# Centring three of four token tiles on GpSimd, and turning them one batch later

## The chip, the cores and the metric

The kernel runs on one core of one Trainium2 chip. The metric is the device time of one execution in microseconds (us); of several executions the median is taken. The engines are TensorE (PE in the profile; its weight loads are PEld), VectorE (DVE), ScalarE (ACT), GpSimd (POOL) and SyncE (SP), which issues the transfers.

## The reference

One transformer-like block over 2048 tokens of width 512. The tokens are normalised without gain or bias, then go two ways: through sliding-window attention (32 heads of 16, each query sees itself and the 255 tokens before it) and through a gated feed-forward of width 1792. The two are multiplied and added to the input.

```python
def _layernorm(x, axis=-1, eps=1e-5):
    m = jnp.mean(x, axis=axis, keepdims=True)
    v = jnp.var(x, axis=axis, keepdims=True)
    return (x - m) / jnp.sqrt(v + eps)
...
    xn = _layernorm(x, axis=-1)
    s = _A_ref(xn, A_wqkv, A_wo)
    g = _silu(_B_ref(xn, B_w1, B_w3, B_w2))
    return x + s * g
```

## The kernel before, in words

The 2048 tokens are worked on in four tiles of 512 (`t` = 0 to 3), each of four blocks of 128 tokens. For precision, operands of the large products are held as a high and a low float16 part, and three products are summed (high by high, high by low, low by high). Splitting a float32 array is shared out: ScalarE scales it (L342) and copies the high part (L343), and GpSimd subtracts to get the low part, in two halves of 256 columns (`halves`, L336 to L339). GpSimd makes so the low parts of the feed-forward weights, of the hidden values (L1050 and L1051, read by the down products of L1242), and of the attention output.

Before a tile can be used, its tokens are prepared (`prepare`, L425). For each block, `stats` (L435) takes mean and variance on VectorE. `rstd` (L440) makes the reciprocal root for all four blocks: three short operations on VectorE, then, for the second to fourth tile, ten on GpSimd (L463 to L472). `centre` (L474) subtracts the mean and multiplies with the reciprocal root, in place, one 128x512 operation of VectorE a block (L475). For the first tile `turn` (L478) then transposes on TensorE. For the others `turn_beside` (L502) does: each block is turned in two pieces, each piece a few small matmuls against an identity (L513) into free columns of a PSUM bank that a score matmul is using anyway, from which VectorE copies the high part (L522) and subtracts the low part (L523).

The attention's work is cut into 32 units (`units`), two for each of 16 pairs of tile and group of eight heads, and each unit into five batches (`batches`, L1427). A batch holds score matmuls of a first pass (L661), whose row maxima VectorE takes (L675), and score matmuls of a second pass (L741), to which VectorE adds masks (L748) and of which ScalarE takes the exponential (L751). Between batches, `spread` (L1456) lays the dense work: gate and up products (L1017), projections (L593), values (L563), down products (L1242 or, in the last two tiles, L1160), and the output projection (L1294).

What sets the order: TensorE issues in the order in which the program is written. The other engines' instructions are put in order at build time by a scheduler, from priorities and from when it thinks their inputs are there; `tc.issue_after` ties instructions behind one of the same engine. On the chip each engine's queue is first in, first out.

The preparation of tiles 2 to 4 is spread over batches. `prepare_beside` (L529) makes a list `work`: statistics (in pairs of blocks for the second tile, one block at a time for the others), the reciprocal roots, then the centring in the same portions, then `turns`. The list goes into `behind`, and each batch takes one entry (L1449 to L1451), tied behind the batch's last row maximum if it is on VectorE. `turns` is called twice, once from this list and once by a call outside it, and the second of the two calls puts the eight turning pieces of the tile into `besides`. From there `part` of the first pass (L650) takes them, as a rule one for a batch, and more than one while the units of the first three pairs of tile and group run.

Buffers of 512 float32 columns come from a pool of 55 slots (`take` and `give`); a token block's slot is given back when its second piece has been turned (L515).

Of the kernel before, what the change touches and what calls it, by code (L numbers as in the profile page):

```python
# [15 lines left out]
ALU = mybir.AluOpType  # L16
# [67 lines left out]
def tile_block(ctx: ExitStack, tc: tile.TileContext, x, wqkv, wo, w1, w3, w2, out):  # L84
    nc = tc.nc
# [58 lines left out]
    def later(n, f):  # L144
        made_so_far[0] += 1
        queue.append((now[0] + n, made_so_far[0], f))
# [274 lines left out]
    lasts = {}  # L421
# [3 lines left out]
    def prepare(t):  # L425

        mv = lnpool.tile([P, 4, 2], F32, name="mv")
        rs = lnpool.tile([P, 4], F32, name="rs")
        xts = {}
# [42 lines left out]
            pool.tensor_mul(rs[:, b0:b1], sq, r0)  # L472

        def centre(b):  # L474
            lasts["centre"] = nc.vector.tensor_scalar(xts[b], xts[b], mv[:, b, 0:1], rs[:, b:b + 1],  # L475
                                                      op0=ALU.subtract, op1=ALU.mult)

        def turn(b):  # L478
            if t not in X:
# [22 lines left out]
        def turn_beside(b, n, s):  # L502
# [15 lines left out]
            def rest():  # L518
# [5 lines left out]
                if n:  # L524
                    turned[t] = turned.get(t, 0) + 1
            return rest
        return load, stats, rstd, centre, turn if t == 0 else turn_beside

    def prepare_beside(t, more=0):  # L529


        load, stats, rstd, centre, turn = prepare(t)
        made = [(0, lambda b=b: load(b)) for b in range(4)]
        pairs = [(0, 1), (2, 3)] if t == 1 else [(b,) for b in range(4)]
        work = [lambda bs=bs: [stats(b) for b in bs] for bs in pairs]
        work.append(lambda: rstd(0, 4))
        work += [lambda bs=bs: [centre(b) for b in bs] for bs in pairs]
        ready = []

        def turns():  # L540

            ready.append(0)
            if len(ready) == 2:
                besides.extend(lambda s, b=b, n=n: turn(b, n, s) for b in range(4) for n in (0, 2))
        work.append(turns)
        made.append((0, lambda: later(more, lambda: behind.extend(work))))
        return made, turns
# [296 lines left out]
    def load(t, f):  # L844
        if t:
            a = [take(F16) for _ in range(2)]
            WF[t, f] = [a, None]
            for k in range(2):
                lasts["load"] = nc.sync.dma_start(a[k], dW1[f, k])
            return  # L850
        RAW[f] = raw = [take(F32) for _ in range(2)]
        for k, w in enumerate((w1, w3)):
            lasts["load"] = nc.sync.dma_start(raw[k].rearrange("p (c f) -> p c f", f=P),
                              w[:, f * P:(f + 1) * P].rearrange("(c p) f -> p c f", p=P))
# [475 lines left out]
    def feed_forward():  # L1330
# [4 lines left out]
        for t in range(NT):  # L1335
            for f in range(FB):
# [27 lines left out]
                if f == FB - 4 and t + 2 < NT:  # L1364
                    first, second = prepare_beside(t + 2, 8)
                    pieces += first
# [214 lines left out]
    for n in range(len(units)):  # L1581
        t = n // 8
# [8 lines left out]
        b = n % 8 - (2 if t < 3 else 3)  # L1591
# [6 lines left out]
    for n, u in enumerate(units):  # L1598
        if n == 0:
            first, second = prepare_beside(1, 2)  # L1600
            later(10, lambda: run(first[:4]))
        if n == 1:
            run(first[4:])
            second()
        if n == 6:
            wout[0]()
        if n == 7:
            wout[1](2)
            beside_scores(12, lambda s: then(s, wout[2](s), lambda: later(2, lambda: wout[3](2)), lambda: later(3, out_scale)))
        want += a_unit - other[n]  # L1610
        mine = more(want)

        lists = in_groups(beside[n]), in_groups(mine)
        both = sorted([((i + 0.5) / len(l), k, i) for k, l in enumerate(lists) for i in range(len(l))])
        spread(batches(n, u, units[n + 2] if n + 2 < len(units) else None), [piece for _, k, i in both for piece in lists[k][i]])
        k = n // 2 + 2
        if n % 2 == 0 and k < len(tiles):
            later(1, lambda k=k: fetch(*tiles[k]))
# [33 lines left out]
```

## Time and profile before

| | |
|---|---|
| runs of the kernel | 818.03, 820.48 and 822.88 us; median 820.48 us |
| the profiled execution | 817.94 us, of which the span of the profile is 816.1 us |
| granted clock of TensorE | 0.998 of full speed |
| TensorE busy | 98% of the span, 9176 matmuls |
| VectorE, ScalarE, GpSimd busy | 78%, 48%, 45% |

The profile shows one execution. Its views name an instruction by engine, line of the kernel, operation, and tiles written and read. A timeline gives, for each instruction or each run of like ones, its start and its duration in us, and in brackets how long the engine stood idle before it and whom it was waiting for. Since one instruction can begin while the one before it writes its last results, the durations of neighbours overlap a little. The chain of work that ended last is followed back from the end: at each step to what released the instruction, or to the one before it on its engine. A table of windows gives the busy time of each engine within a stretch.

### The profile page before, as it was taken

What the parts mean: (1) busy time and instruction counts of PE and PEld (TensorE: products, weight loads), DVE (VectorE), ACT (ScalarE), POOL (GpSimd) and SP (SyncE); (2) the same over time, 40 slices, a digit from 0 to 9 for tenths busy, and PEclk for the clock granted to TensorE, in tenths of its full rate; (3) what the DMA queues carried; (4) which work ended last, traced back from release to release, by engine and by line L of the source; (5) the groups of instructions that cost most, each with busy time, mean ns of one, the idle gap of its engine ahead of it and who ended that gap; (6) DMA issues with size and microseconds to landing.
All of it is one profiled execution on the core that took longest, in us unless ns stands there. A gap on an engine that the chain in (4) does not pass through costs nothing.

```text
span 816.1 us, 23926 instructions
## 1 busy us (share of the span) xinstructions
PE 796.3 (98%) x9176; PEld 404.3 (50%) x9176; DVE 633.0 (78%) x2033; ACT 395.1 (48%) x595; POOL 371.0 (45%) x656
## 2 busy tenths in 40 slices
PE   8998989999999999999999999999999999999997
PEld 4443444444444444444444454456544654466464
DVE  8787688888898767787988888777677886875537
ACT  6879486563536544345444334344344234344411
POOL 2237266232329536344444355530246376650671
PEclk9999999999999999999999999999999999999999
DMA  9979665664742486747536362755553653325511
GB/s 283 257 246 309 211 192 169 202 209 146 217 137 85 133 251 196 232 132 217 160 124 186 91 185 82 210 153 151 165 151 85 169 160 109 88 72 178 159 37 64
DMA packets 109923, 134.71 MB, mean 165 GB/s; under 512 B 18736, under 2 KB 64752, under 8 KB 109808
## 3 DMA queue, kind: packets, MB, share of 16 engines
q1 hardware_dynamic: 109520, 132.66, 55.0%
q8 instruction: 72, 1.18, 0.6%
q10 hardware_dynamic: 288, 0.52, 0.2%
q14 instruction: 43, 0.35, 0.1%
HBM read 91.75 MB, written 37.09 MB: 158 GB/s over the span
## 4 chain that ended last, share of the span: by engine, by line
PE 71%; DVE 13%; ACT 6%; DMA 4%; issue 3%; POOL 2%; SPq 0%; DVEq 0%; POOLq 0%; ACTq 0%
PE m L1017 27%; PE m L1242 8%; PE po L769 7%; PE m L1160 7%; PE m L593 6%; PE s L741 5%; DVE junk L675 4%; PE m L1294 3%; PE m L563 3%; PE s L661 2%; DVE s L748 2%; PE po L661 1%; ACT slot L342 1%; ACT pt L751 1%; ACT slot L343 1%
## 5 line engine op out<-in xcount | busy, mean ns | idle before, releaser
L1017 PE MATMUL m<-XH,slot 128*128 128x512 f16 x896 | 267.3, 380 | 1.5 <-DVE slot L614 1.0
L751 ACT ACTIVATE pt<-s,es 128x1024 f32<-128x1024 f32 x152 | 167.7, 1114 | 195.3 <-DVE s L748 191.3
L339 POOL TENSOR_TENSOR slot<-slot,slot 128x256 f16<-128x256 f32 (+1 forms) x178 | 117.8, 691 | 207.1 <-ACT slot L1050 77.9
L1017 PEld LDWEIGHTS <-slot 128*128 128x128 f16 x1344 | 124.8, 98 | 155.6 <-issue 11.9
L1017 PE MATMUL m<-XL,slot 128*128 128x512 f16 x448 | 169.8, 379 | 0.0
L748 DVE TENSOR_TENSOR s<-s,MK 128x256 f32<-128x256 f32 (+2 forms) x280 | 118.7, 434 | 49.9 <-PE s L741 46.3
L675 DVE CUSTOM_DVE_ANT_0 junk<-s,MW 128x320 bf16<-128x320 f32 x276 | 133.9, 485 | 17.7 <-PE s L661 11.2
L675 DVE CUSTOM_DVE_ANT_0 junk<-po,MW 128x320 bf16<-128x320 f32 x172 | 83.4, 485 | 4.3
L1242 PE MATMUL m<-slot,slot 128*128 128x512 f16 x336 | 80.9, 386 | 2.5 <-POOL slot L339 2.1
L769 PE MATMUL po<-pt,V 64*32 64x320 f32 (+4 forms) x2880 | 77.2, 342 | 0.8 <-DVE pp L304 0.8
L593 PE MATMUL m<-XH,slot 128*128 128x512 f16 x240 | 70.9, 380 | 1.2 <-DVE slot L614 0.6
L1160 PE MATMUL m<-slot,slot 128*128 128x256 f16 x588 | 68.4, 273 | 0.3 <-DVE slot L1036 0.3
L1075 POOL TENSOR_TENSOR slot<-slot,slot 128x256 f16<-128x256 f32 x98 | 65.2, 678 | 1.2
L1032 ACT ACTIVATE slot<-m,sgs 128x512 f32<-128x512 f32 x56 | 38.3, 683 | 54.8 <-PE m L1017 44.2
L1160 PEld LDWEIGHTS <-slot 128*128 128x128 f16 x588 | 56.2, 98 | 11.8 <-issue 3.1
L769 PEld LDWEIGHTS po<-pt,V 64*32 64x32 f32 x2880 | 50.4, 106 | 23.2 <-PE s L513 0.9
L1036 DVE SCALAR_TENSOR_TENSOR slot<-slot,m 128x512 f32<-128x512 f32 x56 | 38.3, 684 | 29.7 <-ACT slot L1032 29.7
L741 PE MATMUL s<-qa,KA 50*64 50x320 f16 (+3 forms) x1472 | 58.6, 259 | 0.5 <-DVE os L784 0.2
L593 PEld LDWEIGHTS <-slot 128*128 128x128 f16 x384 | 35.7, 98 | 44.5 <-issue 3.2
L741 PEld LDWEIGHTS <-KA 50*64 50x64 f16 x1472 | 30.3, 105 | 52.2 <-issue 30.8
L339 POOL TENSOR_TENSOR on<-on,rb 128x256 f32<-128x256 f32 x32 | 24.4, 785 | 61.3 <-DMA rb<-de 48.1
L1242 PEld LDWEIGHTS <-slot 128*128 128x128 f16 x336 | 31.1, 99 | 42.6 <-issue 9.8
(188 smaller groups left out, 1120.7 us busy)
## 6 DMA issues: line engine op xcount, KB each, us to landing
slot<-dW SPq DMA_DIRECT2D x98, 256.0 KB
slot<-in_B_w_dram SPq DMA_DIRECT2D x56, 256.0 KB
slot<-dFold SPq DMA_DIRECT2D x48, 256.0 KB
dW<-slot SPq DMA_DIRECT2D x42, 256.0 KB
slot<-in_A_x_dram SPq DMA_DIRECT2D x30, 256.0 KB
KA<-dK SPq DMA_DIRECT2D x24, 288.0 KB
qa<-dQ SPq DMA_DIRECT2D x32, 192.0 KB
slot<-dWQ SPq DMA_DIRECT2D x24, 256.0 KB
```

The source lines that it names most:

```text
L339: op(out[:, c], a[:, c], b[:, c])
L593: nc.tensor.matmul(cell["pp"], w[:, (a * NC + c) * P:(a * NC + c + 1) * P], b[:, c, :], start=(c, i) == parts[0][0], stop=(c, i) == parts[ ...
L675: lasts["maximum"] = nc.vector.tensor_tensor_reduce(out=junk[:, :n], in0=s[:, r, :n], in1=mask, scale=1.0, scalar=NEG, op0=ALU.add, op1=AL ...
L741: nc.tensor.matmul(s[64 * h:64 * h + 64, r, o:o + 64 * n], ka[rows, 2 * p + a, 64 * (m + 4):64 * (m + 5)], qa[rows, 2 * p + a, 64 * (m + k ...
L748: nc.vector.tensor_add(v, v, MK[:, kind, of:of + n, :].unsqueeze(1).to_broadcast([P, 2 * len(which), n, 64]))
L751: lasts["exp"] = nc.scalar.activation(pt, s, AF.Exp, scale=es)
L769: nc.tensor.matmul(cell["po"][32 * i:32 * i + 32, h, 64 * (m + k):64 * (m + k + n)], V[64 * h:64 * h + 64, (4 * t + m // 2) % VB, hd * VW: ...
L1017: nc.tensor.matmul(cell[k], w[:, (a * NC + c) * P:(a * NC + c + 1) * P], b[:, c, :], start=c == 0 and i == 0, stop=c == NC - 1 and i == 2)
L1032: nc.scalar.activation(sg, cell[0], AF.Tanh, scale=sg_scale[:, f:f + 1])
L1075: nc.gpsimd.tensor_sub(lo, view, hi)
L1160: nc.tensor.matmul(cell["ps"][:, c], made[:, f:f + P], wj[:, g:g + 256], start=j == j0 and c == 0 and n == 0, stop=j == j1 - 1 and n == 2, ...
L1242: nc.tensor.matmul(ps, hh[:, a * TW + b * P:a * TW + (b + 1) * P], w[:, c * D:(c + 1) * D], start=f == f0 and i == 0, stop=f == f1 - 1 and ...
```

## The change

For the second to fourth tile (`t` of 1 to 3) `centre` is issued on GpSimd in place of VectorE, as two operations of 256 columns for each block: 24 operations of 128x256 in place of 12 of 128x512. The first tile keeps VectorE. And the list `work` gets an entry that does nothing, between the last centring and `turns`, so that the turning pieces are offered one batch later.

```diff
         def centre(b):
-            lasts["centre"] = nc.vector.tensor_scalar(xts[b], xts[b], mv[:, b, 0:1], rs[:, b:b + 1],
-                                                      op0=ALU.subtract, op1=ALU.mult)
+            if t == 0:
+                lasts["centre"] = nc.vector.tensor_scalar(xts[b], xts[b], mv[:, b, 0:1], rs[:, b:b + 1],
+                                                          op0=ALU.subtract, op1=ALU.mult)
+                return
+            for c in (slice(0, 256), slice(256, 512)):
+                nc.gpsimd.tensor_scalar(xts[b][:, c], xts[b][:, c], mv[:, b, 0:1], rs[:, b:b + 1],
+                                        op0=ALU.subtract, op1=ALU.mult)
...
         work += [lambda bs=bs: [centre(b) for b in bs] for bs in pairs]
+        work.append(lambda: None)
         ready = []
```

## The prediction

> **What bounds the kernel now.** I read the page first: the engines' busy time, then the chain of work that ended last.
>
> ```profile
> span 816.1 us, 23926 instructions
> ...
> PE 796.3 (98%) x9176; PEld 404.3 (50%) x9176; DVE 633.0 (78%) x2033; ACT 395.1 (48%) x595; POOL 371.0 (45%) x656
> ...
> PE 71%; DVE 13%; ACT 6%; DMA 4%; issue 3%; POOL 2%; SPq 0%; DVEq 0%; POOLq 0%; ACTq 0%
> ```
>
> TensorE is busy for 796.3 of 816.1 us. The change takes nothing from TensorE, so all that it can win lies in the 19.8 us in which TensorE stands idle, and only in those of them that the centring causes. The chain has 13% of VectorE, so somewhere VectorE sets the pace. To find where, I took the busy time by windows (columns: window and its length, then PE, PEld, DVE, ACT and POOL busy with counts, clock, DMA share, GB/s), and then TensorE's timeline, keeping the instructions with idle time before them.
>
> ```profile
> 115.00:120.00 5.00, 3.54 (x32) 1.50 (x24) 4.86 (x20) 4.03 (x10) 1.51 (x4) 1.00 0.65 202
> 120.00:125.00 5.00, 3.99 (x64) 2.31 (x64) 3.93 (x17) 5.00 (x9) 4.30 (x7) 1.00 0.77 260
> 125.00:130.00 5.00, 4.36 (x55) 2.14 (x53) 4.16 (x12) 3.94 (x11) 2.07 (x4) 1.00 0.63 218
> 130.00:140.00 10.00, 9.18 (x151) 4.89 (x150) 9.16 (x37) 7.22 (x11) 5.98 (x10) 1.00 0.52 164
> 140.00:160.00 20.00, 20.00 (x258) 10.06 (x257) 15.31 (x58) 9.72 (x18) 5.69 (x11) 1.00 0.54 177
> 160.00:180.00 20.00, 18.64 (x160) 8.22 (x166) 17.07 (x64) 14.69 (x23) 10.93 (x18) 1.00 0.65 215
> ...
> 395.00:425.00 30.00, 29.95 (x387) 14.12 (x392) 26.82 (x87) 14.41 (x18) 10.15 (x24) 1.00 0.43 125
> ```
>
> ```profile
> 116.53 0.22 PE L694 MATMUL s<-identh,NM 64*64 64x64 f16 x2 [1.09 <-DVE NM L688]
> ...
> 118.62 0.59 PE L593 MATMUL m<-XH,slot 128*128 128x512 f16 x2 [0.37 <-DVE slot L1036]
> ...
> 121.44 0.30 PE L661 MATMUL s<-KA,qa 48*64 48x256 f16 x4 [1.01 <-ACT pt L751]
> ...
> 127.47 0.33 PE L661 MATMUL po<-KA,qa 48*64 48x320 f16 x4 [0.64 <-DVE XL L523]
> ...
> 133.34 2.04 PE L769 MATMUL po<-pt,V 64*32 64x320 f32 x72 [0.82 <-DVE pp L304]
> ...
> 190.39 1.46 PE L1242 MATMUL m<-slot,slot 128*128 128x512 f16 x6 [0.40 <-DVE slot L614]
> ```
>
> Between 115 and 134 us TensorE loses 1.09 + 0.37 + 1.01 + 0.64 + 0.82 = 3.93 us, nearly all on VectorE's account. This is where the second tile's tokens are prepared. From 140 to 160 us TensorE is never idle, from 160 to 180 us it loses 1.36 us, and one wait of 0.40 us follows at 190.39 us. Now the centring itself: its summary over the run (durations as least, median and most, in ns), VectorE's timeline around the second and third tile's, and the summary for the fourth tile's four.
>
> ```profile
> L475 DVE TENSOR_SCALAR slot<-slot,mv,rs x16: 535/544/1102, 9.5 to 421.4; 128x512 f32<-128x512 f32 x16
> ```
>
> ```profile
> 109.64 0.87 DVE L475 TENSOR_SCALAR slot<-slot,mv,rs 128x512 f32<-128x512 f32 x1 [0.40 <-POOL rs L472]
> ...
> 110.51 0.82 DVE L475 TENSOR_SCALAR slot<-slot,mv,rs 128x512 f32<-128x512 f32 x1
> ...
> 114.95 0.97 DVE L475 TENSOR_SCALAR slot<-slot,mv,rs 128x512 f32<-128x512 f32 x1
> 115.84 0.64 DVE L688 SCALAR_TENSOR_TENSOR NM<-M,NM 128x16 f16<-128x16 f32 x1
> ...
> 116.47 0.54 DVE L475 TENSOR_SCALAR slot<-slot,mv,rs 128x512 f32<-128x512 f32 x1
> ...
> 184.74 0.17 DVE L688 SCALAR_TENSOR_TENSOR NM<-M,NM 128x16 f16<-128x16 f32 x1
> ...
> 188.64 1.10 DVE L475 TENSOR_SCALAR slot<-slot,mv,rs 128x512 f32<-128x512 f32 x1
> ```
>
> ```profile
> L475 DVE TENSOR_SCALAR slot<-slot,mv,rs x4: 542/709/893, 408.7 to 421.4; 128x512 f32<-128x512 f32 x4
> ```
>
> The third centring of the second tile stands directly ahead of L688, for which TensorE then waits 1.09 us. The one at 188.64 us takes 1.10 us and stands ahead of the L614 that TensorE waits for at 190.39 us. The fourth tile's end by 422 us, in a stretch, 395 to 425 us, in which TensorE is idle for 0.05 of 30 us.
>
> **The change, part by part.** *Removed from VectorE:* twelve operations. In the second tile 0.87 + 0.82 + 0.97 + 0.54 = 3.20 us between 109.64 and 117.0 us, and with them the 0.40 us in which VectorE stood waiting for GpSimd's reciprocal root. In the third and fourth tile the only wait of TensorE that has a centring ahead of it is that at 190.39 us.
>
> How much of this reaches TensorE? The waits at 116.53 and 118.62 us (1.46 us) are on VectorE alone, and VectorE will be over 2 us early there: they go. The one at 121.44 us is for ScalarE's exponential, so ScalarE's own gaps decide:
>
> ```profile
> 113.21 0.62 ACT L1050 CAST slot<-slot 128x512 f16<-128x512 f32 x1 [0.56 <-DVE slot L1041]
> 114.02 1.11 ACT L751 ACTIVATE pt<-s,es 128x1024 f32<-128x1024 f32 x1 [0.19 <-DVE s L748]
> ...
> 118.02 1.33 ACT L342 ACTIVATE slot<-slot,sw 128x512 f32<-128x512 f32 x2 [0.94 <-DVE sw L930]
> ```
>
> ScalarE waits for VectorE 0.56 + 0.19 + 0.94 = 1.69 us ahead of that exponential and is otherwise busy. It can come at most 1.7 us early, so TensorE, counted at 121.44 us, gains 1.7 us and not 1.09 + 0.37 + 1.01 = 2.47: ScalarE is what is late next. Behind it, the waits of 0.64 and 0.82 us stand behind VectorE's copies of turned columns and the work next to them, which the change moves but keeps. I leave them as they are. The third tile gives its 0.40 us, the fourth nothing: 1.7 + 0.4 = 2.1 us.
>
> *Added to GpSimd:* 24 operations of 128x256, one input, float32 to float32, two scalars a partition. The trace of before has no such operation. The nearest rows, by line with their mean in ns, and GpSimd's queue at the place:
>
> ```profile
> L1074 POOL CAST slot<-slot 128x256 f16<-128x256 f32 x56 | 21.6, 401 | 0.8
> ...
> L1099 POOL TENSOR_TENSOR slot<-slot,slot 128x256 f32<-128x256 f32 x14 | 10.2, 728 | 1.1
> ```
>
> ```profile
> 109.56 6.89 POOL L339 TENSOR_TENSOR slot<-slot,slot 128x256 f16<-128x256 f32 x10
> 119.94 2.56 POOL L339 TENSOR_TENSOR slot<-slot,slot 128x256 f16<-128x256 f32 x4 [3.49 <-ACT slot L343]
> 123.20 2.56 POOL L339 TENSOR_TENSOR slot<-slot,slot 128x256 f16<-128x256 f32 x4 [0.70 <-ACT slot L1050]
> 126.94 1.30 POOL L339 TENSOR_TENSOR slot<-slot,slot 128x256 f16<-128x256 f32 x2 [1.18 <-ACT slot L343]
> 133.59 1.31 POOL L339 TENSOR_TENSOR slot<-slot,slot 128x256 f16<-128x256 f32 x2 [5.34 <-ACT slot L1050]
> ```
>
> I put one at 0.40 to 0.73 us and take 0.45, near the row with one input. Eight for a tile are 3.2 to 5.8 us, 3.6 by my value. Who waits behind them? The low parts that the ten, four, four and two L339 make, the last of which TensorE's down products read:
>
> ```profile
> 137.42 3.99 PE m L1242 x18
> ```
>
> With no idle time at all, GpSimd would be through the operations up to 126.94 us at 109.56 + 6.89 + 2.56 + 2.56 + 1.30 + 5.8 = 128.7 us by the dear end, 0.5 us later than the 128.2 us of now, and 137.42 less 1.7 us is still 7 us away. Its idle 3.49 + 0.70 + 1.18 + 5.34 us are the cover; if it were gone, each us on GpSimd would be one on TensorE. So this costs nothing.
>
> *Beside each other:* centring took 0.54 us alone and up to 1.10 us beside GpSimd, L688 0.17 us and 0.64 us. GpSimd's new operations may hold up VectorE's short ones in the same way. One such hold-up costs 0.64 - 0.17 = 0.47 us; I count one on the path, 0.5 us, with bounds of nothing and eight (one for each new operation of the second tile, 3.8 us).
>
> Here a rule speaks against the change. The Trainium skill, Perfetto Trace Analysis, Optimizing Scalar/DVE Operations, warns that moving operations between these two engines might not help, since they share an SBUF read port. The rows above agree that they hold each other up; by the rule the sum would be about nothing, which is the first rival below.
>
> *The turning, one batch later:* the pieces move with their copies:
>
> ```profile
> 121.55 0.43 PE L513 MATMUL s<-identf,slot 64*64 64x64 f32 x16
> ...
> 124.65 0.42 DVE L523 TENSOR_TENSOR XL<-s,XH 128x256 f16<-128x256 f32 x1
> ...
> 127.63 0.40 PE L513 MATMUL po<-identf,slot 64*64 64x64 f32 x16
> ```
>
> One batch is here 127.63 - 121.55 = 6.1 us. The first turn would thus be due at 127.63 less the 1.7 us won, about 126 us. Its block is centred, even behind all ten operations of 6.89 us, at 109.56 + 6.89 + 2 x 0.73 = 117.9 us: the matmuls that TensorE issues in program order do not wait. No DMA is issued in the step; slots of tokens come free a batch later, which I put at nothing, between -1 and +1 us, as what is loaded next may land earlier or later in another slot.
>
> **The sum:** 2.1 - 0.5 = 1.6 us. On the profiled execution, 817.94 - 1.6 = 816.3 us (span 814.5). The median of the runs, 820.48 us, lies 2.5 us above that execution; taking the same off the median gives **818.9 us**.
>
> **Rivals.** *First, the relief is eaten (no change, 820.0 to 821.0 us, about 820.5).* GpSimd's operations hold up VectorE for as long as the centring took: four to five hold-ups of 0.47 us undo 2.1 us. For it speaks L688's 0.64 us, against it that most of VectorE's time at this place goes into operations that show one duration throughout, beside GpSimd or not.
>
> *Second, the whole stretch comes free (814.8 us).* VectorE sets the pace from before 115 to 134 us. If its 3.2 us and the move of the copies also remove the waits of 0.64 and 0.82 us, and the lead lasts through the 1.36 us lost from 160 to 180 us, TensorE regains 3.93 + 1.36 + 0.40 = 5.7 us. For it speaks that from 140 to 160 us VectorE has 4.7 us free for the moved copies; against it, ScalarE at 5.00 of 5.00 us from 120 to 125 us.
>
> *Third, the moved copies stall TensorE (slower, about 825 us).* A piece brings VectorE two copies of 0.42 us, 0.84 us. They move into the batches from 127 to 152 us, where the down products' results also have to be taken. From 140 to 160 us VectorE is free for 4.69 of 20 us, about 1.2 us for a batch of 5 us. While a batch's free time is above 0.84 us, a piece fits. From below that on, TensorE waits for the bank as at 133.34 us, up to 0.82 us for each of eight pieces, 6.6 us. Less the 2.1 us won, it is 4.5 us slower, 825.0 us. For it speaks 9.16 of 10 us busy from 130 to 140 us.
>
> *Fourth, the delay does nothing* in the third and fourth tile, if the call of `turns` outside the list is the later one; then the pieces stay where they are. By the sum above it changes the time by nothing and belongs to my forecast.
>
> **How the numbers follow.** My forecast (won 0.5 to 4.1 us, 816.4 to 820.0) gets 0.48, the first rival 0.20, the second 0.14, the third 0.18. The range reaches from the second to the third rival, 814.5 to 825.0 us, which leaves out what lies beyond the two. Half a per cent, 4.1 us, is about what a measurement of this kernel can tell from no change. Faster by more than that is the second rival and the edge of the forecast, 0.18; slower the third, 0.18; the rest, 0.64, lies within it.
>
> **What would show it.** Right: no wait of 1.09 us for L688 in the second tile's stretch, TensorE's idle time from 115 to 134 us down from 3.9 to some 2.2 us, ScalarE as the releaser of what is left; L475's 12 operations gone from VectorE and 24 on GpSimd at 0.40 to 0.73 us; the first L513 near 126 us with no idle before it. Wrong: TensorE waiting for GpSimd at L513 or L1242, GpSimd's new operations above 0.73 us, short operations of VectorE stretched to 0.6 us more often than now, or TensorE waiting for L522 and L523 between 127 and 152 us. If the total moves by over 4 us with none of these, a reordering elsewhere did it, and the prediction is wrong in its place.

## The result, and the profile after

The changed kernel takes 831.1 us (median of four runs, 829.3 to 832.32) and the kernel before 819.36 us (818.03 to 822.88): the ratio, which is taken over all the runs and is not the quotient of the medians, is 1.0135, with a 95% interval of 1.0107 to 1.0163. Predicted were 818.9 us and a range that ended at 825.0. The profiled execution took 829.3 us. Its page:

```profile
span 827.5 us, 23949 instructions
...
PE 798.4 (96%) x9176; PEld 404.9 (49%) x9176; DVE 635.3 (77%) x2021; ACT 394.4 (48%) x595; POOL 398.2 (48%) x680
...
PE 75%; DVE 8%; DMA 5%; ACT 4%; issue 4%; POOL 3%; SPq 1%; DVEq 0%; POOLq 0%; ACTq 0%
```

The span grew by 11.4 us: TensorE is idle for 29.1 us instead of 19.8, and busy for 2.1 us longer with the same 9176 matmuls. VectorE lost twelve operations and is yet busier than before, 635.3 us for 633.0; the time in which an operation of VectorE is held up counts as busy. In the chain its share fell from 13% to 8%, while transfers rose from 4% to 5%.

Where is it lost? The same small matmul (L694 before, L700 after) runs in every unit, so its start times, laid side by side, show who is ahead. TensorE's timeline, before:

```profile
94.39 0.19 PE L694 MATMUL s<-identh,NM 64*64 64x64 f16 x2
...
141.64 0.19 PE L694 MATMUL s<-identh,NM 64*64 64x64 f16 x2
...
410.20 0.19 PE L694 MATMUL s<-identh,NM 64*64 64x64 f16 x2
...
432.75 0.19 PE L694 MATMUL s<-identh,NM 64*64 64x64 f16 x2
...
741.43 0.22 PE L694 MATMUL s<-identh,NM 64*64 64x64 f16 x2
```

And after, with the one at 113.23 us that answers to 116.53 us before:

```profile
92.72 0.19 PE L700 MATMUL s<-identh,NM 64*64 64x64 f16 x2
...
113.23 0.20 PE L700 MATMUL s<-identh,NM 64*64 64x64 f16 x2
...
146.94 0.19 PE L700 MATMUL s<-identh,NM 64*64 64x64 f16 x2
...
415.50 0.19 PE L700 MATMUL s<-identh,NM 64*64 64x64 f16 x2
...
442.55 0.19 PE L700 MATMUL s<-identh,NM 64*64 64x64 f16 x2
...
752.11 0.22 PE L700 MATMUL s<-identh,NM 64*64 64x64 f16 x2
```

The changed kernel is 3.30 us ahead at 113 us. Then it loses 8.6 us in the second tile (it is 5.30 us behind at 147 us), nothing in the third (still 5.30 behind at 415 us), 4.5 us in the fourth (9.80 behind) and another 0.9 us up to 752 us (10.68).

The new operations, from the summary of their line:

```profile
L480 POOL TENSOR_SCALAR slot<-slot,mv,rs x24: 1213/1218/1254, 108.0 to 421.1; 128x256 f32<-128x256 f32 x24
```

One takes 1.22 us, 2.7 times the 0.45 us taken. All eight of the second tile stand in one run, and behind them eighteen low parts, GpSimd's timeline:

```profile
108.03 9.65 POOL L480 TENSOR_SCALAR slot<-slot,mv,rs 128x256 f32<-128x256 f32 x8
117.65 11.32 POOL L339 TENSOR_TENSOR slot<-slot,slot 128x256 f16<-128x256 f32 x18
```

From 108.03 to 128.97 us GpSimd never pauses. Before, its first low parts began at 109.56 us; now at 117.65. Two things follow. The first is on VectorE (its timeline; L261 makes four columns of sums of squares into bfloat16):

```profile
118.19 10.81 DVE L261 CAST sb<-ssq 128x4 bf16<-128x4 f32 x1 [0.72 <-ACT sqa L249]
128.91 0.42 DVE L754 TENSOR_TENSOR s<-s,MK 128x256 f32<-128x256 f32 x1
```

An operation on four columns stands until GpSimd's run ends, and VectorE's masks and row maxima stand behind it. The second is on SyncE, its waits from 104 to 134 us (whom a line waited for: us in all, times, longest), after:

```profile
SPq L1029 <- POOL slot L339: 12.2, 2, 11.4
```

Before, the line (L1023 there) waited:

```profile
SPq L1023 <- POOL slot L339: 2.8, 2, 1.8
```

A weight store that waits for its low part (L1029) stands 11.4 us in SyncE's queue; nothing is issued from 104.8 to 118.98 us, and behind the store come transfers that have nothing to do with weights, SyncE's timeline, after:

```profile
103.99 0.82 SPq L643 DMA_DIRECT2D KA<-dK  x2
118.98 1.60 SPq L1029 DMA_DIRECT2D dW<-slot  x2
...
122.38 2.45 SPq L797 DMA_DIRECT2D on<-os  x4
124.88 0.53 SPq L798 DMA_DIRECT2D dd<-os  x1
...
127.27 0.33 SPq L813 DMA_DIRECT2D dr<-dd  x1
```

Before, `dr<-dd`, which brings the attention's sums back for the reciprocal, was issued 7.1 us earlier, SyncE's timeline, before:

```profile
120.14 0.37 SPq L807 DMA_DIRECT2D dr<-dd  x1
```

What TensorE has of all this, its timeline, after:

```profile
117.60 0.30 PE L667 MATMUL s<-KA,qa 48*64 48x256 f16 x4 [0.74 <-ACT pt L757]
...
130.26 0.64 PE L747 MATMUL s<-qa,KA 50*64 50x320 f16 x10 [8.23 <-DVE M L681]
...
131.71 0.66 PE L518 MATMUL po<-identf,slot 64*64 64x64 f32 x16
132.35 1.01 PE L1023 MATMUL m<-XH,slot 128*128 128x512 f16 x2
...
435.97 0.50 PE L747 MATMUL s<-qa,KA 50*64 50x256 f16 x8 [3.10 <-DMA qa<-dm]
```

The idle 8.23 us end at 130.26 us. At 435.97 us the fourth tile has its own: TensorE waits for a transfer, `qa<-dm`. The pair of matmuls at 132.35 us takes 1.01 us where it takes 0.59 us elsewhere (L593 at 118.62 us before). The windows show the clock that goes with it (columns as in the prediction; the clock is the third number from the end), after:

```profile
125.00:130.00 5.00, 0.00 (x0) 0.00 (x0) 5.00 (x6) 0.03 (x1) 3.97 (x7) 0.58 0.69 223
130.00:135.00 5.00, 4.50 (x45) 2.31 (x46) 3.71 (x13) 4.61 (x10) 1.30 (x2) 0.50 0.82 265
...
435.00:440.00 5.00, 4.03 (x21) 1.64 (x22) 2.19 (x6) 1.11 (x1) 4.92 (x10) 0.66 0.98 250
```

After the idle stretch the clock is 0.50 until 135 us, and around the wait of 3.10 us it is 0.66; before, it was 1.00 in the same work. So both waits are paid a second time in slow matmuls. From the small matmul at 92.72 us (94.39 before) to that at 146.94 us (141.64) TensorE is busy 44.90 us for 43.25, and from 435.97 to 442.55 us (427.80 to 432.75) 6.58 us for 4.95: 1.65 and 1.63 us more.

### The profile page after: what moved, and what is told of

It reads as the page before. It is cut to its first block, busy times and chain, and to the rows that moved or that the text cites. A ratio compares the mean times of both kernels' runs of the same rounds, so it can differ in the third digit from the quotient of the medians.

```text
span 827.5 us, 23949 instructions
## 1 busy us (share of the span) xinstructions
PE 798.4 (96%) x9176; PEld 404.9 (49%) x9176; DVE 635.3 (77%) x2021; ACT 394.4 (48%) x595; POOL 398.2 (48%) x680
## 3 DMA queue, kind: packets, MB, share of 16 engines
q8 instruction: 72, 1.18, 0.6%
## 4 chain that ended last, share of the span: by engine, by line
PE 75%; DVE 8%; DMA 5%; ACT 4%; issue 4%; POOL 3%; SPq 1%; DVEq 0%; POOLq 0%; ACTq 0%
PE m L1023 28%; PE m L1248 9%; PE po L775 8%; PE m L1166 8%; PE m L599 7%; PE s L747 5%; PE m L1300 3%; PE m L569 3%; PE s L667 2%; DVE junk L681 2%; DMA slot<-in_B_w_dram 2%; PE po L667 1%; DVE s L754 1%; ACT pt L757 1%; POOL slot L339 1%
## 5 line engine op out<-in xcount | busy, mean ns | idle before, releaser
L1023 PE MATMUL m<-XH,slot 128*128 128x512 f16 x896 | 269.9, 383 | 1.7 <-DVE slot L620 1.0
L1023 PEld LDWEIGHTS <-slot 128*128 128x128 f16 x1344 | 125.6, 98 | 158.4 <-issue 16.2
L1023 PE MATMUL m<-XL,slot 128*128 128x512 f16 x448 | 171.0, 382 | 0.0
L1248 PE MATMUL m<-slot,slot 128*128 128x512 f16 x336 | 79.0, 380 | 2.1 <-POOL slot L339 2.1
L1042 DVE SCALAR_TENSOR_TENSOR slot<-slot,m 128x512 f32<-128x512 f32 x56 | 38.3, 684 | 30.7 <-ACT slot L1038 30.6
L1166 PEld LDWEIGHTS <-slot 128*128 128x128 f16 x588 | 56.2, 98 | 11.4 <-issue 3.0
```

The lines of the kernel that those rows point to most:

```text
L1023: nc.tensor.matmul(cell[k], w[:, (a * NC + c) * P:(a * NC + c + 1) * P], b[:, c, :], start=c == 0 and i == 0, stop=c == NC - 1 and i == 2)
L1166: nc.tensor.matmul(cell["ps"][:, c], made[:, f:f + P], wj[:, g:g + 256], start=j == j0 and c == 0 and n == 0, stop=j == j1 - 1 and n == 2, ...
L1248: nc.tensor.matmul(ps, hh[:, a * TW + b * P:a * TW + (b + 1) * P], w[:, c * D:(c + 1) * D], start=f == f0 and i == 0, stop=f == f1 - 1 and ...
```

## The experiments

The theory at the start was that the eight operations in one run hold up VectorE and SyncE in two places; its rivals were that the delay does it, that the price of an operation does it wherever and however the eight are placed, and that one of the two holds alone makes the loss. Each run is named by its edit. A minus and a plus stand for lines of the kernel that it starts from.

**The delay alone** (the kernel before with only the empty entry).

```diff
+        work.append(lambda: None)
```

> The centring stays on VectorE as before, only the empty entry is added, so that the second to fourth tile are turned one batch later. Theory A (the loss comes from GpSimd's centring, which is 1.22 us for 256 columns and runs eight in a row): no loss here, 817 to 821 us. Rival B (the turned columns' copies, moved one batch later, stall TensorE): most of the 11 us loss is here, 826 to 832 us.

Measured: 818.09 us beside 818.05, ratio 0.9995 (0.9966 to 1.0023). The later turning alone costs nothing that shows, so the loss is the centring's.

**The changed kernel without the delay.**

```diff
-        work.append(lambda: None)
```

> The changed kernel without the empty entry, so that GpSimd centres and the tokens are turned at the batch of before. Theory A (the centring's price and what stands behind it make the loss, the later turning does not matter): 829 to 833 us, as the change. Rival (without the delay TensorE also waits at the turning for the third portion, which GpSimd ends late): 833 to 838 us, with waits at the identity matmuls of the second tile.

Measured: 829.71 us, 1.0121 (1.0067 to 1.0175). L261's cast again stood 10.81 us. Both directions agree: the delay plays no part that shows.

**A cheaper operation** (the changed kernel with GpSimd copying instead of centring; the centring of these tiles is left out).

```diff
-                nc.gpsimd.tensor_scalar(xts[b][:, c], xts[b][:, c], mv[:, b, 0:1], rs[:, b:b + 1],
-                                        op0=ALU.subtract, op1=ALU.mult)
+                nc.gpsimd.tensor_copy(xts[b][:, c], xts[b][:, c])
```

> The changed kernel, with GpSimd's 24 centrings replaced by as many copies in place of the same columns; it leaves out the centring of the second to fourth tile, so only the time counts. Theory A (the price of 1.22 us is what failed): at 0.4 us a piece, the price that the prediction assumed, the loss goes: 815 to 820 us, with no cast of 10 us and no late transfers. Rival (any eight operations there, of whatever price, break the order): 824 to 832 us.

Measured: 818.39 us, 0.9982 (0.9949 to 1.0014). The new operations, by the summary of their line:

```profile
L480 POOL COPY slot<-slot x24: 396/400/404, 96.1 to 399.3; 128x256 f32<-128x256 f32 x24
```

At 0.40 us an operation the time is within half a per cent of before, if anything faster. But a copy doesn't wait for the reciprocal root: the second tile's eight run from 96.06 to 102.38 us, in pauses of GpSimd and ahead of the root, while the run of low parts starts at 108.29 us. So the run shows that eight operations a tile, when they are cheap and early, lose nothing; it doesn't test the price at the place where the centring stands, between the root and the low parts. Even then the lead isn't kept to the end. TensorE's timeline of this run:

```profile
426.79 0.51 PE L746 MATMUL s<-qa,KA 50*64 50x256 f16 x8 [1.45 <-DMA qa<-dm]
...
533.98 2.75 PE L1299 MATMUL m<-slot,slot 128*128 128x512 f16 x12 [0.69 <-DVE slot L1041]
```

A lead of 2.2 us at 410 us is given back in these two places, where the kernel before waits 0.24 us at most: TensorE came sooner, its inputs did not.

**What a GpSimd operation costs** (a probe behind the kernel before: forms of 128x256, each four times or more, and VectorE's short operations beside runs of them).

```diff
+    def form_a():
+        g.tensor_scalar(res[:, h], src[:, h], two[:, 0:1], two[:, 1:2], op0=ALU.subtract, op1=ALU.mult)
...
+    for f in (form_a, form_b, form_c, form_d, form_e):
+        for _ in range(4):
+            f()
...
```

> The kernel before, and after its last store a row of single costs: on GpSimd four operations each of 128x256 with two scalars from SBUF (form a), two constants (b), one scalar from SBUF (c), 128x512 with two scalars (d), one constant (e); then runs of GpSimd operations without a gap, with one small VectorE operation that may start after the first of them: 18 and 9 subtractions with a cast of 128x4, 9 tensor_scalars with the cast, 18 copies with the cast, 18 subtractions with an add of two SBUF inputs, 18 subtractions with a centring of 128x512. What is added leaves the result as it is. If the price of 1.22 us is the operation's, a takes 1.2 us, d twice the slope; if it comes from the scalars in SBUF, b and e take 0.4 us. Theory S (a gapless run of GpSimd subtractions starves VectorE to its end): the cast takes some 11 us beside 18, some 5 us beside 9. Rival (one instruction holds the other up at most): under 1 us in all.

Measured, the summaries of its lines (least, median and most, in ns): two scalars from SBUF, two constants, one scalar from SBUF, two scalars over 512 columns, one constant, a subtraction of two arrays, a copy:

```profile
L1647 POOL TENSOR_SCALAR slot<-slot,two x4: 1220/1221/1380, 814.5 to 818.6; 128x256 f32<-128x256 f32 x4
L1650 POOL TENSOR_SCALAR slot<-slot x4: 1068/1068/1070, 819.9 to 823.4; 128x256 f32<-128x256 f32 x4
L1653 POOL TENSOR_SCALAR slot<-slot,two x4: 917/922/925, 824.5 to 827.6; 128x256 f32<-128x256 f32 x4
L1656 POOL TENSOR_SCALAR slot<-slot,two x4: 2066/2074/2076, 828.6 to 835.1; 128x512 f32<-128x512 f32 x4
L1659 POOL TENSOR_SCALAR slot<-slot x4: 847/848/857, 837.3 to 840.1; 128x256 f32<-128x256 f32 x4
L1667 POOL TENSOR_TENSOR slot<-slot,slot x63: 667/668/728, 841.2 to 908.1; 128x256 f16<-128x256 f32 x63
L1673 POOL CAST slot<-slot x18: 396/400/400, 873.5 to 881.3; 128x256 f16<-128x256 f32 x18
```

Each of these forms of tensor_scalar is dearer than a subtraction of two arrays: 0.85 us with one constant, 0.92 with one scalar from SBUF, 1.22 with two operations and two such scalars. The 1.22 us are the form's own price and no contention of this place. Twice the columns cost 2.07 us. The short cast took at most 0.62 us beside runs of subtractions, so theory S fails here.

**The cast on ScalarE** (the changed kernel).

```diff
-            with tc.issue_after(lasts["emptied"].ins) if "emptied" in lasts else nullcontext():
-                cast()
+            nc.scalar.copy(sb, ssq)
```

> The changed kernel, with the small casts of the sums of squares (L261) that are issued beside the scores given to ScalarE. Theory A1 (in the second tile this cast sits for 10.8 us behind a gapless run of GpSimd subtractions, and everything on VectorE behind it): the 8.2 us wait of TensorE at 130 us goes, or shrinks to what the next VectorE operation that reads SBUF alone (the reciprocal of 128x32) suffers; 820 to 825 us, the fourth tile's loss of 4.5 us remaining. Rival C (TensorE waits there for GpSimd's late low parts or for data, and the cast only shows it): the wait stays with another releaser, 828 to 832 us.

Measured: 826.64 us, 1.0094 (1.0067 to 1.0122). No operation stands on VectorE any more, and three quarters of the second tile's wait stay, TensorE's timeline of this run:

```profile
132.84 1.44 PE L1247 MATMUL m<-slot,slot 128*128 128x512 f16 x3 [6.12 <-DVE slot L1041]
...
434.07 0.51 PE L746 MATMUL s<-qa,KA 50*64 50x256 f16 x8 [4.06 <-DMA qa<-dm]
```

L1041 stands on VectorE behind the reciprocal, and the reciprocal behind the transfer that SyncE issued late; VectorE's timeline:

```profile
131.24 0.35 DVE L817 RECIPROCAL dr<-dr 128x32 f32<-128x32 f32 x1 [7.41 <-DMA dr<-dd]
```

The two effects lie on top of each other: with the cast out of the way, the second ends almost as late. The time lies between the two forecasts, 820 to 825 and 828 to 832 us.

**The cast as a maximum of two inputs, and as a reduction** (the changed kernel, same place in VectorE's queue).

```diff
-                cast()
+                lasts["cast"] = nc.vector.tensor_tensor(sb, ssq, ssq, op=ALU.max)
```

> The changed kernel with the one VectorE cast that stood 10.81 us in it (L261, 128x4 to bf16) written as a maximum of the array with itself, an operation of two inputs, at the same place of VectorE's queue. If the form of the cast, a copy, is what let GpSimd's run of eighteen hold it, then the maximum takes 0.1 to 0.9 us beside the same run, no operation of VectorE stands for 10 us there, and the time is about that of the run in which ScalarE made the cast, 826 to 827 us, the rest of the loss being the reciprocal's late data (TensorE's wait for L1042's slot or the like, 5 to 6 us at 132 us, and some 4 us at 434 us). If the place in the queue or what it waits for is what counts, the maximum stands for 9 to 11 us as the cast did, until GpSimd's run ends near 129 us, and the time is that of the changed kernel, 829 to 832 us.

```diff
-                cast()
+                lasts["cast"] = nc.vector.tensor_reduce(sb, ssq.unsqueeze(2), axis=AX.X, op=ALU.max)
```

> The changed kernel with the one VectorE cast that stood 10.81 us in it (L261, 128x4 to bf16) written as a maximum over an axis of one element, at the same place of VectorE's queue: one input from SBUF and no copy. Written as a maximum of two inputs from SBUF it still stood 10.79 us. The Trainium skill, SBUF - State Buffer, Who interferes with whom, has it that casts, tensor_scalars and operations with two inputs from SBUF need the ports that VectorE shares with GpSimd, and that a reduction never does. If what stands is an operation that needs the shared ports, the reduction takes 0.1 to 0.3 us beside the same run of eighteen subtractions, and the time is that of the run in which ScalarE made the cast, 826 to 827 us, the rest being the reciprocal's late data at 132 us and the wait of some 4 us at 434 us. If anything of SBUF stands there, or what it waits for counts, it takes 9 to 11 us, until GpSimd's run ends near 129 us, and the time is 829 to 832 us.

Measured: 830.6 us, 1.0137 (1.0107 to 1.0168) for the maximum, and 829.64 us, 1.0109 (1.0079 to 1.0138) for the reduction. VectorE's timeline, the maximum:

```profile
118.59 10.79 DVE L265 TENSOR_TENSOR sb<-ssq 128x4 bf16<-128x4 f32 x1 [0.72 <-ACT sqa L249]
```

and the reduction:

```profile
118.73 0.16 DVE L265 TENSOR_REDUCE sb<-ssq 128x4 bf16<-128x4 f32 x1 [0.72 <-ACT sqa L249]
```

The same data at the same place of the same queue, beside a run of GpSimd that ends at 129.4 us with the maximum and at 130.8 us with the reduction: two inputs from SBUF stand 10.79 us, a reduction 0.16 us. So the kind of the operation decides here whether it is held. The Trainium skill, SBUF — State Buffer, Who interferes with whom, says that casts, tensor_scalars and operations with two SBUF inputs can contend for a port pair shared with GpSimd, and that reductions never do; these three forms agree. It also says that whoever issues first gets the pair for the whole instruction; that one of GpSimd's eighteen subtractions, 0.63 us of 11.32, holds VectorE up would fit this, the 10.8 us through all of them go beyond it. The time came down less than I expected (826 to 827): TensorE then waited 6.37 us for L1042's slot, and in the profiled execution it lost a further 4.5 us near 545 us, over 100 us behind the last centring, for a reason that I did not find.

**Seventeen different outputs** (a second probe: one run of GpSimd writing into different places, as the kernel's does, to see whether that makes the hold long).

```diff
...
+    def run_beside(op, n, beside, same=False):
+        op(first[:, h])
+        beside()
+        for i in range(n - 1):
+            j = 0 if same else i
+            op(outs[j // 4][:, 256 * (j % 4):256 * (j % 4) + 256])
...
```

> The kernel before, and after its last store runs of GpSimd operations whose outputs are 17 different places, so that none has to wait for the one before it; in the first probe all wrote one place. Beside each run one VectorE operation that may start after the first: a cast of 128x4 float32 to bf16 beside 18 and beside 9 subtractions, the same beside 18 subtractions into one place, beside 9 tensor_scalars, beside 18 copies; then beside 18 subtractions an add with two SBUF inputs, a tensor_scalar of 128x32, a centring of 128x512. What is added leaves the result as it is. Theory S2 (independent subtractions follow each other so closely, 0.63 us apart, that VectorE's cast gets no turn before the run ends): the cast takes about 11 us beside 18, 5 us beside 9, and under 1 us where all write one place. Rival (the cast of 10.8 us has another cause): under 1 us everywhere.

Measured: the cast took 0.62 us beside such a run, and an addition of four columns, beside eighteen subtractions that took 11.32 us, 0.61 us, VectorE's timeline:

```profile
863.02 0.61 DVE L1659 TENSOR_TENSOR tiny<-slot,tiny 128x4 f32<-128x4 f32 x1 [0.85 <-POOL slot L1647]
```

Beside a run of the same length VectorE waits here for about one operation of GpSimd, and theory S2 fails too. The kernel before agrees with the probes: beside its run of ten subtractions from 109.56 us on, the centring at 110.51 us took 0.82 us (the prediction's rows). Why VectorE waits in the changed kernel for the whole run stays open.

**Spreading the centring** (the changed kernel; a small copy on VectorE, one a block, hands GpSimd the block's scalar, so that the blocks are released batch by batch).

```diff
+        rt = lnpool.tile([P, 4], F32, name="rt")
...
+            nc.vector.tensor_copy(rt[:, b:b + 1], rs[:, b:b + 1])
...
-                nc.gpsimd.tensor_scalar(xts[b][:, c], xts[b][:, c], mv[:, b, 0:1], rs[:, b:b + 1],
+                nc.gpsimd.tensor_scalar(xts[b][:, c], xts[b][:, c], mv[:, b, 0:1], rt[:, b:b + 1],
```

> The changed kernel with one more small VectorE copy for each block (128x1, the reciprocal root), which stands in the batch in which the centring was written; GpSimd's centring reads this copy and so is let go batch by batch, not eight in a row. Theory A (the bunching, not the 1.22 us as such, makes both losses): no cast of 10 us, no wait of 3 us in the fourth tile, and VectorE's relief remains: 816 to 822 us. Rival E (1.22 us a piece on GpSimd is too much anyhow, its low parts come late wherever it stands): 825 to 832 us.

Measured: 825.47 us, 1.0076 (1.0046 to 1.0105). The cast takes 0.42 us, but TensorE's timeline has

```profile
131.18 2.72 PE L1250 MATMUL m<-slot,slot 128*128 128x512 f16 x6 [5.07 <-DVE slot L1044]
...
432.22 0.50 PE L749 MATMUL s<-qa,KA 50*64 50x256 f16 x8 [3.47 <-DMA qa<-dm]
```

The theory that the bunching of the eight is the whole cause falls: the time is at the lower end of the rival's forecast. But it is a part, since the loss went down from 1.35 to 0.76%, with intervals that just don't overlap. In the second tile the eight, 9.68 us in all, stood in three runs between the low parts, and `dr<-dd` was issued at 125.96 us, 1.3 us earlier than in the changed kernel and still 5.8 us later than before. In the fourth tile six of the eight stood in one run of 7.22 us all the same, so that there the spreading was not tested.

**Two tiles, one tile.** The second tile's centring back on VectorE, and then the fourth's too, so that only the third tile's is on GpSimd:

```diff
-            if t == 0:
+            if t <= 1:
```

> The changed kernel, but the second tile's tokens are centred on VectorE as before; third and fourth on GpSimd. Theory A: TensorE's position at the third tile equals that of before within 1 us, and the fourth tile still loses some 4.5 us near 436 us, where eight centrings in a row hold back a low part whose store holds SyncE's queue: 822 to 826 us. Rival D (the fourth tile's loss follows from slots that changed hands in the second tile): nothing is lost at 436 us, 817 to 821 us.

```diff
-            if t == 0:
+            if t != 2:
```

> The changed kernel with only the third tile's centring on GpSimd; the second and fourth tile's stay on VectorE, the turning stays a batch later. If the loss is made where GpSimd's run stands ahead of low parts for which SyncE's queue waits (second and fourth tile), and the third tile's run has nothing of that kind behind it, then the time is that of before, or up to 2 us below it, 816 to 819 us, no wait of TensorE over 2 us stands at 130 or 430 us, and the eight operations of 1.22 us cost nothing. If 9.7 us on GpSimd cost by themselves wherever they are, a third of the loss shows: 821 to 824 us.

Measured: 822.6 us, 1.0036 (1.0003 to 1.007), with one great wait left, TensorE's timeline of the first of the two:

```profile
430.56 0.27 PE L747 MATMUL s<-qa,KA 50*64 50x256 f16 x1 [3.67 <-DMA qa<-dm]
```

and 820.4 us, 1.0014 (0.998 to 1.0049), for the third tile alone, within what can be told from no change, though its ten runs spread from 815.44 to 827.26 us and the median lies between the two forecasts. With the second tile back on VectorE its loss is gone, clear of the intervals (1.0036 against 1.0135), and the fourth tile's wait stays. The third tile's eight operations cost nothing that shows, though six of them stood in one run of 7.25 us. What the fourth tile's eight cost can't be told from the times, as the intervals of the two runs overlap; and the run with the third tile alone has a smaller wait at the same transfer, TensorE's timeline of it:

```profile
429.91 0.27 PE L747 MATMUL s<-qa,KA 50*64 50x256 f16 x1 [1.85 <-DMA qa<-dm]
```

So a part of that wait can come without GpSimd's centring in this tile. In the changed kernel it is SyncE again, its waits from 400 to 440 us, after:

```profile
SPq L999 <- POOL slot L994: 9.2, 2, 7.2
```

and before:

```profile
SPq L993 <- POOL slot L988: 7.3, 3, 4.7
```

A store of folded weights (L999), ahead of `dm<-mt` and `qa<-dm` in the queue, waits 7.2 us for its low part where it waited 4.7. It is issued at 426.35 us instead of 418.35; 5.30 of these 8.0 us are what the kernel was behind already. TensorE then waits 3.10 us for `qa<-dm`, where it waited 0.24 us before, and the slow matmuls behind the wait take 1.63 us more: together the 4.5 us that the tile loses.

**SyncE's queue, relieved in two ways** (both from the kernel with the cast on ScalarE). First, the stores of `dW1` for two of the weight blocks are left out, and loads of those blocks read two blocks earlier:

```diff
-                    nc.sync.dma_start(dW1[f, k], w)
+                    if f not in (8, 9):
+                        nc.sync.dma_start(dW1[f, k], w)
...
-                lasts["load"] = nc.sync.dma_start(a[k], dW1[f, k])
+                lasts["load"] = nc.sync.dma_start(a[k], dW1[f - 2 if f in (8, 9) else f, k])
```

> The changed kernel with the small casts on ScalarE, and with the stores of the gate and up weights of columns 8 and 9 left out (later tiles load the weights two columns before in their place, so only the time counts). Theory Q (in the second tile SyncE's queue stands at these stores, which wait for GpSimd's late low parts, and the attention's transfers behind them come late to VectorE): the transfers of the attention's sums go out by 115 us in place of 123 us, and of the 6 us that TensorE waited near 132 us, most go: 820 to 824 us. Rival (the transfers are held by slots that GpSimd still reads): 825 to 828 us.

Measured: 828.28 us, 1.0111 (1.0054 to 1.0168). SyncE stands as long as before, its waits from 104 to 134 us:

```profile
SPq L903 <- POOL slot L338: 12.1, 1, 12.1
```

A load (L903) that waited for GpSimd took the stores' place, and `dr<-dd` was issued at 129.81 us, no earlier than with the stores (128.39 us). That the stores alone hold the queue is wrong; the next transfer that waits for GpSimd holds it as long. Second, one group's transfers of the attention's sums, issued by ScalarE:

```diff
-                nc.sync.dma_start(dd[4 * p:4 * p + 4, :], os[DH::32, :])
+                (nc.scalar if (t, g, p) == (0, 0, 1) else nc.sync).dma_start(dd[4 * p:4 * p + 4, :], os[DH::32, :])
...
-        nc.sync.dma_start(dr, dd.rearrange("h (b c) -> (h b) c", c=32))
+        (nc.scalar if (t, g) == (0, 0) else nc.sync).dma_start(dr, dd.rearrange("h (b c) -> (h b) c", c=32))
```

> The changed kernel with the small casts on ScalarE, and with the transfers of one group's sums (the second half of the first tile's first group: four of the values, one of the denominators, and its return to VectorE) issued by ScalarE in place of SyncE. Theory Q2 (SyncE's queue, in order, holds these transfers behind one that waits for GpSimd): the reciprocal gets its data before VectorE comes to it, and the wait of 6 us of TensorE near 132 us goes, 819 to 823 us, about 5 us under the 826.6 us of the small casts alone. Rival (the data are late for another reason, or the next wait on GpSimd takes its place): 825 to 829 us.

Measured: 833.4 us, 1.0162 (1.0115 to 1.0208). Now ScalarE stood behind GpSimd, its timeline:

```profile
124.20 0.69 ACT L1037 ACTIVATE slot<-m,sgs 128x512 f32<-128x512 f32 x1 [10.93 <-POOL slot L338]
```

The time is above both forecasts. This settles nothing about the queue: the wait for GpSimd moved to another engine.

**Another engine for the centring** (the kernel before, with tiles two to four centred on ScalarE from a bias made by two small operations of GpSimd).

```diff
+            pool.tensor_mul(nb, mv[:, :, 0], rs)
+            pool.tensor_scalar(nb, nb, -1.0, None, op0=ALU.mult)
...
+            if t:
+                nc.scalar.activation(xts[b], xts[b], AF.Identity, bias=nb[:, b:b + 1], scale=rs[:, b:b + 1])
+                return
```

> The kernel before, with the centring of the second to fourth tile on ScalarE (one 128x512 operation a block with scale and bias, the bias made by two more 128x4 operations on GpSimd), turned as before. VectorE is relieved as by the change, GpSimd is not loaded, ScalarE gets 12 operations of some 0.65 us. If VectorE's relief is worth the 3.3 us that the changed kernel was ahead at 113 us, and ScalarE has room: 815 to 818 us. If ScalarE, or VectorE's wait for the reciprocals' data, takes it back: 818 to 821 us.

Measured: 825.06 us, 1.0069 (1.0042 to 1.0096), above both forecasts, with TensorE waiting 1.98 us for ScalarE's exponential at 115.66 us and 3.01 us for VectorE (L620) at 191.94 us. No version was found that beats the kernel before.

## Why the prediction was wrong

**The relief (1.7 us by ScalarE as the next limit).** Right, and on the small side. The wait of 1.09 us on L688 is gone, and the wait that stood at 121.44 us stands at 117.60 us, with ScalarE's exponential as its releaser as foretold. That is 3.84 us earlier. Of these, 1.67 us were there at 94.39 us already, ahead of the centring; 2.17 us are this stretch's. The 0.4 us of the third tile came too: TensorE has no wait there. That the relief would last to the end was assumed and not argued; the run with copies shows it given back at 427 and 534 us.

**The price (0.45 us, 0.40 to 0.73).** This is the step that failed first. I bounded a tensor_scalar with two scalars by a copy and a subtraction of the same size, since each has one or two inputs. The form's price doesn't go by inputs: it measured 1.22 us, outside both ends. The eight took 9.7 us and not 3.2 to 5.8.

**"So this costs nothing".** The second step that failed, and the one that made the price matter. I asked who waits behind GpSimd and named the down products, with 7 us of cover, from the end of the queue. The eighteenth low part came at 128.97 us instead of 125.76 (123.20 + 2.56, in the prediction's rows), which the down products don't feel. But the first came 8 us later, and those that wait for the first are stores and loads on SyncE. The prediction asked only for DMAs that the moved step itself issues, and there are none. The transfers of others that wait for GpSimd were in the trace of before, 2.8 us of waiting in the second tile and 7.3 us in the fourth.

How far is this shown? That the centring on GpSimd makes the loss and the delay doesn't, and that most of it is made in the second tile, is shown by the runs. The fourth tile's share is read from the traces. How much of the loss is the price is not shown: no run put operations of 0.45 us at the place of the centring, where even they would have pushed the first low parts back by 3.6 us, as an estimate from the prediction's own sum. That SyncE's late transfer is what the reciprocal and, behind it, L1041 wait for is read from the traces (11.4 us of waiting, 7.41 us, 6.12 us, one behind the other). Four runs without the long cast agree: `dr<-dd` is issued at 125.96 (spreading), 127.83 (reduction), 128.39 (cast on ScalarE) and 129.81 us (stores left out), and TensorE goes on 4.5 to 5.2 us behind it. No run freed that queue alone, so this link is argued from the order of the queue and not tested.

**Contention (one hold-up of 0.47 us, at most eight).** The place was right and the size wrong. It was one hold-up, of 10.81 us, in which a run of eighteen subtractions stood together that pauses had parted before. The first rival had this mechanism and priced it as short stretches. The hold itself adds little to the time: without it the loss of 1.35% is 0.94% (ScalarE's cast) or 1.09% (the reduction), some 2 to 3 us of 11, with intervals that overlap, since SyncE's late sums lie beneath it.

**The delay and the turning.** Right: no cost, either way it was tested. The first turn came at 131.71 us and not near 126, only because all of TensorE stood for 8.23 us ahead of it. The third rival, which carried the slower side of my range, was wrong: copies of turned columns are not what TensorE waits for in the great waits. The time came out slower than that rival by another mechanism.

**What would show it wrong** named the right thing, GpSimd's operations above 0.73 us, and priced no case for it. With 1.22 us in the sum as an upper bound, the eight take 9.8 us, more than GpSimd's idle 3.49 + 0.70 + 1.18 us in that stretch; that would have been a reason to give the slower side more than 0.18.

## What to carry to other kernels

When work is moved onto an engine with idle time, look up who reads the first of what its queue makes next, and not only the last: in-order transfer queues that wait for it pass the delay on to transfers of another part of the kernel. Bound a form that the trace doesn't show by more than the nearest shapes: an operation with scalars isn't a copy with something added. And whether idle time is a reserve depends on who waits behind it: in the second tile a run of eight operations cost most of the loss, in the third six of eight in one run cost nothing that shows.

## What the runs showed of the hardware

GpSimd's 128x256 tensor_scalar took 0.85 us with one constant, 1.07 with two, 0.92 with one scalar from SBUF, 1.22 with two, against 0.40 for a copy and 0.67 for a subtraction of two arrays. A VectorE cast or two-input operation on four columns stood 10.8 us beside a run of eighteen of GpSimd's operations, a reduction in its place 0.16 us; beside a probe's run it stood 0.61 us, and what makes the difference is open. After 8.23 us without a matmul TensorE's clock was 0.50 from 130 to 135 us, and a matmul pair took 1.01 us for 0.59; around a wait of 3.10 us it was 0.66 from 435 to 440 us.
